# Talking-heads attention with a Fourier mix: the score and premix matmuls in 64x32 tiles, a new step order, and the order at the seam of two stages

## The chip, the cores and the metric

The kernel runs on one core of one Trainium2 chip. The metric is the device time of an execution in microseconds; each kernel is run several times and the median is compared. All data is float32.

## The reference, cut to what matters

```
B, NH, S, D = 8, 12, 448, 64
scores = q @ k.T / sqrt(D)                      # per batch and head, S x S
scores = einsum('bhij,hg->bgij', scores, w_pre) # premix: the 12 heads are mixed
attn   = softmax(scores, axis=-1)
attn   = einsum('bhij,hg->bgij', attn, w_post)  # postmix: mixed again
x      = (attn @ v), heads side by side         # B x S x 768
u      = x + real(fft(fft(x, axis=1), axis=2))
un     = (u - mean(u)) / sqrt(var(u) + 1e-6)    # over the last axis
out    = u + relu(un @ w_ch1) @ w_ch2           # 768 -> 3072 -> 768
```

## The kernel before, in words

There are two phases. `mix_phase` is the attention and the Fourier mix; `ffn_phase` is the norm and the two large products.

**The attention's step.** A batch is cut into 24 steps; there are TOT = 192 steps. Each step mixes 4 groups of 5 query rows, for all 12 heads (60 = KR rows on the partitions). The work of one row group passes through the following operations, several steps apart:

- `emit_qk` (L432): the scores of a block of query rows and two heads in each half of the array. They go to PSUM tiles `ms` and are copied by ScalarE to `Sb`. There is about one such group in every step.
- `emit_gather` (L451): four DMAs on SP's queue bring `Sb` into `Kr`, with heads and rows on the partitions. It runs LG = 4 steps ahead.
- `emit_premix` (L464): the first mixing, `Kr` times the constant `kw1`, into the PSUM tiles `mx`, LM = 2 steps ahead. There are four matmul calls in the four 64x64 quarters of the array.
- `emit_max` (L474) on VectorE, `emit_exp` (L481) on ScalarE, which also adds up the denominators, and `emit_scale` (L490) with the reciprocal on VectorE and the product on GpSimd.
- `emit_postmix` (L499): the second mixing, into `po`. There are eight matmul calls, each in a 64x32 piece of the array.
- `emit_turn` (L512): VectorE transposes `po` in 32x32 blocks into `Pv`.
- `emit_av` (L522): the product with v, 28 calls in 64x64 quarters, copied to `XT`. There are 12 in a batch.

Other work is called "full", because it uses the whole array: transposes of q and k (`emit_xpose`, L406), of the attention's output (`emit_x`, L558), and the two products of the Fourier mix, over rows (`emit_z`, L619) and over columns (`emit_s2`, L639). GpSimd's additions for the Fourier mix are lists of small functions called folds (`fold`, L574).

**What sets the order.** TensorE, VectorE, ScalarE and GpSimd carry out the loop at L750 in the order in which it is written. It calls, step by step: premix, flush (pending PSUM copies), postmix, maxima, exponentials, AV, turn, one operation of the weights' conversion (`wts.deal`), scores, gather, scale, pending stores, folds, full. The tables AT_T, AT_V, AT_QK, AT_AV, AT_X, AT_Z and AT_S (L77 to L85) say in which step of a batch each filling item is due; a step past the batch's end falls into the next batch. ENG (L87) says which engine copies what.

**The seam.** `ffn_phase` loads the first rows of `u` (L867) and the first weights `w1t` (L873). Then a hand-ordered section computes statistics (`stats`, VectorE), the root (`power`, four GpSimd operations, L897 to L900) and the folds left over (`fold_rest`). The next section normalises (`norm`, ScalarE, L908), transposes on TensorE (`turn`, L917, with copies on ScalarE, L919), subtracts (`total`, VectorE, which also issues seven stores of `ub`), and issues the `w2t` loads (L877). The first FFN round also carries the last "full" items between its matmuls. There are 42 rounds, each of `first` (L946) and `second` (L1002).

Of the kernel before, what the change touches and what calls it, by code (L numbers as in the profile page):

```python
# [10 lines left out]
F32 = mybir.dt.float32  # L11
U32 = mybir.dt.uint32
ALU = mybir.AluOpType
ACTF = mybir.ActivationFunctionType
AX = mybir.AxisListType

P = 128
# [13 lines left out]
KR = R * NH  # L31
# [42 lines left out]

AT_T = ((12, 10), (17, 16), (14, 18))  # L77
AT_L = ((-4, -3), (-2, -1), (0, 1), (2, 8), (12, 13), (14, 15))
AT_V = ((3, 4), (5, 6), (7, 7))
AT_QK = ((1, 2, 2), (0, 1, 2), (0, 1, 2), (0, 1, 2),  # L80
         (0, 1, 2), (0, 1, 2), (0, 1, 2), (0, 1, 2))
AT_AV = ((0, 2, 3), (1, 3, 5), (3, 4, 5), (1, 2, 3))
AT_X = (11, 20, 24, 29)
AT_Z = (38, 38, 41, 41)
AT_S = ((40, 44), (53, 55))  # L85

ENG = {("tr", "q", 4): "d", ("tr", "q", 3): "a", ("tr", "k", 4): "d",  # L87
       ("tr", "k", 3): "a", "QK": "aa", "AV": "aa", "X": "aa", "z": "a"}

# [193 lines left out]
def mix_phase(ctx, tc, rest, ident, q, k, v, w_pre, w_post, u_scr, u_rev, wts):  # L285
# [40 lines left out]
    def flush():  # L326
        while pend:
            pend.pop(0)[1]()
# [103 lines left out]
    def emit_qk(n, xx):  # L432

        bk = blocks[n]
        st = batches[bk["b"]]
        if xx == 0:
            bk["Sb"] = psb.tile([P, 6, S], F32, name="Sb", tag="Sb")
        r0 = bk["r0"]
        pss = [ms_tile() for _ in range(2)]
        for y in range(2):  # L440
            lo = r0 + MG * y
            for x in range(2):
                nc.tensor.matmul(  # L443
                    pss[x][64 * y:64 * y + r0 + 64 - lo, :S],
                    st["qT", xx][64 * x:64 * x + 64, y, lo:r0 + 64],
                    st["kT", xx][64 * x:64 * x + 64, y, :],
                    start=True, stop=True)
        return [lambda x=x: copy(ENG["QK"][x], bk["Sb"][:124, 2 * xx + x, :],
                                 pss[x][:124, :S]) for x in range(2)]

# [13 lines left out]
    def emit_premix(T):  # L464
        mx = [pmx.tile([P, 512], F32, name="mx", tag=f"mx{x}") for x in range(2)]
        Kr = steps[T]["Kr"]
        for x in range(2):
            for z in range(2):
                nc.tensor.matmul(mx[x][64 * z:64 * z + 64, :S],  # L469
                                 kw1[64 * x:64 * x + KR, :],  # L470
                                 Kr[64 * x:64 * x + KR, z, :], start=True, stop=True)
        steps[T]["mx"] = mx

    def emit_max(T):  # L474
        nmx = [psm.tile([P, 1], F32, name="nmx", tag=f"nmx{x}") for x in range(2)]
        for x in range(2):
            nc.vector.tensor_reduce(nmx[x][:, :], steps[T]["mx"][x][:, :S],  # L477
                                    axis=AX.X, op=ALU.max, negate=True)
        steps[T]["nmx"] = nmx

    def emit_exp(T):  # L481
        PP = ppp.tile([P, 2, S], F32, name="PP", tag="PP")
        den = psm.tile([P, 2], F32, name="den", tag="den")
        for x in range(2):
            nc.scalar.activation(PP[:, x, :], steps[T]["mx"][x][:, :S], ACTF.Exp,  # L485
                                 bias=steps[T]["nmx"][x][:, :],
                                 accum_out=den[:, x:x + 1])
        steps[T]["PP"], steps[T]["den"] = PP, den

    def emit_scale(T):  # L490
        PP, den = steps[T]["PP"], steps[T]["den"]
# [7 lines left out]
    def emit_postmix(T):  # L499
        po = ppo.tile([P, 2, 512], F32, name="po", tag="po")  # L500
        PP = steps[T]["PP"]
        for y in range(2):
            for c in range(2):
                for z in range(2):
                    o = 64 * y + 32 * c
                    nc.tensor.matmul(po[o:o + 32, z, :S],  # L506
                                     kw2[64 * z:64 * z + KR, y, :],
                                     PP[64 * z:64 * z + KR, :, c * HS:(c + 1) * HS],
                                     start=True, stop=True)
        steps[T]["po"] = po  # L510
# [11 lines left out]
    def emit_av(g, pr):  # L522

        st = batches[g["b"]]
        Pv = g["Pv"]
        rp = _row(Pv)
        nu = GT * 4
        pss = [ms_tile() for _ in range(2)]
        for jb in range(C7):
            for x in range(2):  # L530
                for y in range(2):
                    i = 2 * pr + x
                    nc.tensor.matmul(  # L533
                        pss[y][64 * x:64 * x + 64, :nu * R],
                        st["v", pr][64 * y:64 * y + 64, x, jb * D:(jb + 1) * D],
                        _ap(Pv, 64 * y * rp + 32 * jb + R * i,
                            [[rp, 64], [HS, nu], [1, R]]),
                        start=(jb == 0), stop=(jb == C7 - 1))
        if pr == 0:
            g["XT"] = pxt.tile([P, 6, XW], F32, name="XT", tag="XT")  # L540
        XT = g["XT"]
        rx = _row(XT)
        first, sg, none = PLACE[g["gi"]]

        def done(y):
            rs = _row(pss[y])
            for e in range(2):

                o = MG + first + sg * NB * e
                dst = _ap(XT, (3 * y + pr) * XW + o, [[rx, P], [sg * RS, R], [sg, RS]])  # L550
                src = _ap(pss[y], 60 * e, [[rs, P], [1, R], [R, RS]])
                copy(ENG["AV"][y], dst, src)
            if y == 1 and pr == 2:
                for o in none:
                    nc.gpsimd.memset(XT[:, :, MG + o:MG + o + 1], 0.0)
        return [lambda y=y: done(y) for y in range(2)]

    def emit_x(g):  # L558
# [190 lines left out]
    with tc.manual_schedule(engines={ET.PE, ET.DVE, ET.Activation, ET.Pool}):  # L749
        while s <= TOT - GS + AT_X[-1]:  # L750
            old = len(later)
            n = take("none", s)
            if 0 <= s + LM < TOT:
                emit_premix(s + LM)
            flush()
            if 0 <= s < TOT:
                emit_postmix(s)
            if 0 <= s + LM < TOT:
                emit_max(s + LM)
                emit_exp(s + LM)  # L760
            take("AV", s)
            if 0 <= s < TOT:
                emit_turn(s)
            if s >= 4:
                wts.deal(1)
            take("QK", s)
            if 0 <= s + LG < TOT:
                if any(e[2] is not None and e[2] <= (s + LG) // BS for e in pend):
                    flush()
                emit_gather(s + LG)  # L770
            if 0 <= s + LM < TOT:
                emit_scale(s + LM)
            for _ in range(old):
                later.pop(0)()
            for _ in range(min(len(folds), 1 if n and s > 3 else 2)):
                folds.pop(0)()
            take("full", s)
            s += 1
        flush()
        wts.deal(1000)  # L780
# [32 lines left out]
def ffn_phase(ctx, tc, rest, ident, u_scr, u_rev, wts, ub_scr, out, fold_rest,  # L813
# [61 lines left out]
    def load_w2(c, i):  # L875
        w2[i] = pw2.tile([P, FM, DH], F32, name="w2t", tag="w2t")
        nc.sync.dma_start(out=w2[i][:, :, :], in_=wts.w2[c][i])  # L877
# [33 lines left out]
    def turn(t, x):  # L911
        un = uns.pop(x)
        for y in range(2):
            ps = ps_tile("Q")
            for c in range(NK):
                cc = NK * y + c
                nc.tensor.transpose(ps[:, c * P:(c + 1) * P],  # L917
                                    un[:, cc * P:(cc + 1) * P], ident[:, :])
            nc.scalar.copy(  # L919
                out=ubs[t, UB[y, x // 2]][:, :, (x % 2) * P:(x % 2 + 1) * P],  # L920
                in_=ps[:, :NK * P].rearrange("p (c n) -> p c n", n=P))

    def total(t, n):
        o, a, b = ((4, 6, 0), (5, 2, 4), (6, 2, 6), (3, 1, 5))[n]
# [112 lines left out]
    with tc.manual_schedule(engines={ET.PE, ET.DVE}):  # L1037
        for x in range(NT2):
            norm(0, x)
            turn(0, x)  # L1040
        for n in range(4):
            total(0, n)
        for i in ORDER:
            load_w2(0, i)
        for n in range(NC * NTB):
            c, t = divmod(n, NTB)

            if c + 1 < NC and 0 <= t - (c == 0) < NK + FM:
                wts.add(c + 1, t - (c == 0))
            wts.deal(0)  # L1050
            if c == 0 and t + 2 < NTB:
                load_u(t + 2)
            second(n, first(n))
            wts.deal(1000)
            if n == 0:
                assert not parts
                rest.close()
                pu.append(pool("pu2", side="right"))
                beside.close()
                pps.append(pool("ppy", space=bass.MemoryType.PSUM))  # L1060
# [61 lines left out]
```

## Time and profile before

The median of 17 runs is 2426.83 us (2420.97 to 2434.74). The profiled execution took 2424.31 us; its span from first to last instruction is 2422.5 us, and the granted TensorE clock over it is 0.993 of full speed. The table gives busy times by stretch; PE is TensorE, DVE VectorE, ACT ScalarE, POOL GpSimd.

| stretch (us) | what runs | PE | DVE | ACT | POOL |
|---|---|---|---|---|---|
| 0 to 75 | first loads, first steps | 55.87 | 33.99 | 35.55 | 30.00 |
| 75 to 823 | attention steps | 743.82 | 593.41 | 521.05 | 552.45 |
| 823 to 867 | last steps, seam | 30.68 | 20.00 | 18.28 | 22.16 |
| 867 to 907 | first FFN round with the last mix items | 39.89 | 26.66 | 13.35 | 14.67 |
| 907 to the end | 41 FFN rounds | 1508.85 | 837.38 | 210.35 | 161.59 |

In a timeline line the first number is the start in us, the second the time to the end of the merged instructions, then come engine, source line, operation, output and inputs, shapes and count. Square brackets hold the idle time before it, and what ended that. Matmul ends are modelled, so starts are the safer reading.

### The profile page before, as it was taken

The numbers are of one execution on the slowest core, as the hardware profiler recorded it, in microseconds if no ns is written. First come the engines' busy times: TensorE is split into PE (matmuls) and PEld (weight loads), VectorE is DVE, ScalarE is ACT, GpSimd is POOL, SyncE is SP. The second block draws the span as 40 slices with busy tenths as digits, with TensorE's granted clock in tenths as the row PEclk, the third lists the DMA queues.
The fourth block names the chain that finished last, engine by engine and source line by source line (L and its number), as shares of the span: only waits on it lengthen the run. The fifth ranks groups of instructions, "written<-read, shape, count | busy, mean of one in ns | idle before, by whom it ended". The sixth has DMA issues, their size and how long they took to land.

```text
span 2422.5 us, 48510 instructions
## 1 busy us (share of the span) xinstructions
PE 2379.1 (98%) x18608; PEld 1551.7 (64%) x18608; DVE 1511.5 (62%) x3103; ACT 798.6 (33%) x2059; POOL 780.9 (32%) x1293
## 2 busy tenths in 40 slices
PE   6999999999999899999999999999999999999999
PEld 2445454454554477776777777777777777777776
DVE  3777778788787747785567356635665457533333
ACT  4777667666767542322111111111111110110110
POOL 3687877868676531121111011101110011000000
PEclk8999999999999999999999999999999999999999
DMA  6655554646554457346444444535443644353331
GB/s 146 175 182 162 179 171 155 200 157 191 168 167 146 162 202 215 124 151 232 147 136 153 143 145 135 157 116 170 143 150 98 200 127 146 121 167 114 118 117 52
DMA packets 168596, 372.10 MB, mean 154 GB/s; under 512 B 36750, under 2 KB 90022, under 8 KB 168366
## 3 DMA queue, kind: packets, MB, share of 16 engines
q1 hardware_dynamic: 129038, 260.22, 33.1%
q0 software_dynamic: 33760, 107.40, 15.3%
q8 instruction: 149, 2.44, 0.4%
q10 hardware_dynamic: 5568, 1.38, 0.3%
q14 instruction: 81, 0.66, 0.1%
HBM read 211.98 MB, written 74.34 MB: 118 GB/s over the span
## 4 chain that ended last, share of the span: by engine, by line
PE 94%; DMA 3%; SPq 1%; DVE 1%; ACT 1%; issue 0%; ACTq 0%; DVEq 0%
PE psP L946 18%; PE psP L1002 18%; PE psR L946 9%; PE psR L1002 9%; PE mx L469 7%; PE po L506 7%; PE ms L443 6%; PE ms L533 6%; PE psQ L1002 5%; PE psQ L946 4%; PE ms L647 2%; PE ms L420 2%; DMA Kr<-Sb 1%; PE ms L566 1%; PE ms L631 1%; PE psQ L917 1%
## 5 line engine op out<-in xcount | busy, mean ns | idle before, releaser
L946 PE MATMUL psP<-ub,w1t 128*128 128x256 f32 x2016 | 462.5, 379 | 0.0
L1002 PE MATMUL psP<-w2t,h 128*128 128x384 f32 x1344 | 461.0, 486 | 0.0
L946 PEld LDWEIGHTS psP<-ub,w1t 128*128 128x128 f32 x2016 | 382.8, 190 | 60.7
L207 POOL DMA_DIRECT2D raw<-in_moe_w_ch_dram x120 | 68.9, 574 | 924.5 <-DVE tmp L251 905.7
L1002 PEld LDWEIGHTS psP<-w2t,h 128*128 128x128 f32 x1344 | 254.4, 190 | 165.9
L496 POOL TENSOR_SCALAR PP<-PP,rcp 128x448 f32<-128x448 f32 x384 | 240.7, 636 | 235.6 <-DVE rcp L494 95.7
L477 DVE TENSOR_REDUCE nmx<-mx 128x1 f32<-128x448 f32 x384 | 222.4, 618 | 128.1 <-PE mx L469 125.6
L485 ACT ACTIVATE PP<-mx,nmx 128x448 f32<-128x448 f32 x384 | 240.1, 630 | 171.3 <-DVE nmx L477 159.5
L951 ACT COPY h<-psP 128x512 f32<-128x512 f32 x42 | 24.6, 586 | 764.4 <-PE psP L946 753.2
L1008 DVE TENSOR_TENSOR u<-u,psP 128x384 f32<-128x384 f32 x336 | 183.6, 553 | 141.3 <-PE psP L1002 139.1
L946 PE MATMUL psR<-ub,w1t 128*128 128x256 f32 x1008 | 231.3, 379 | 0.0
L469 PE MATMUL mx<-Kr,kw 60*64 60x448 f32 x1536 | 223.2, 553 | 7.6 <-DMA Kr<-Sb 6.2
L1002 PE MATMUL psR<-w2t,h 128*128 128x384 f32 x672 | 230.5, 486 | 0.0
L517 DVE STREAM_TRANSPOSE Pv<-po 128x896 f32<-128x896 f32 x192 | 212.8, 1108 | 8.7 <-PE po L506 7.5
L957 DVE TENSOR_TENSOR h<-h,psQ 128x512 f32<-128x512 f32 x42 | 28.9, 688 | 298.7 <-PE psQ L946 298.6
L946 PEld LDWEIGHTS psR<-ub,w1t 128*128 128x128 f32 x1008 | 191.4, 190 | 25.9
L324 ACT COPY Sb<-ms 124x448 f32<-124x448 f32 x384 | 184.8, 540 | 18.1 <-PE ms L443 6.4
L506 PE MATMUL po<-PP,kw 60*32 60x448 f32 x3072 | 188.7, 548 | 0.9 <-DVE rcp L493 0.9
L443 PE MATMUL ms<-kT,qT 64*64 64x448 f32 (+1 forms) x1536 | 188.6, 553 | 0.0
L533 PEld LDWEIGHTS ms<-Pv,vv 64*64 64x64 f32 x5376 | 143.8, 133 | 68.3 <-issue 30.7
L1002 PEld LDWEIGHTS psR<-w2t,h 128*128 128x128 f32 x672 | 127.2, 190 | 87.4
L533 PE MATMUL ms<-Pv,vv 64*64 64x120 f32 x5376 | 165.9, 269 | 0.0
(92 smaller groups left out, 2755.5 us busy)
## 6 DMA issues: line engine op xcount, KB each, us to landing
ub<-ub SPq DMA_DIRECT2D x294, 384.0 KB
Kr<-Sb SPq DMA_DIRECT2D x768, 105.0 KB
raw<-in_moe_w_ch_dram POOLq DMA_DIRECT2D x72, 256.0 KB, 3.3
raw<-in_moe_w_ch_dram POOLq DMA_DIRECT2D x48, 384.0 KB, 3.8
w<-wst POOLq DMA_DIRECT2D x126, 128.0 KB, 3.1
w<-wst POOLq DMA_DIRECT2D x84, 192.0 KB, 3.2
w1t<-w SPq DMA_DIRECT2D x42, 384.0 KB
w2t<-w SPq DMA_DIRECT2D x42, 384.0 KB
```

Of the source, the lines that this page charges most:

```text
L324: (nc.scalar.copy if eng == "a" else nc.vector.tensor_copy)(out=out, in_=in_)
L443: nc.tensor.matmul(pss[x][64 * y:64 * y + r0 + 64 - lo, :S], st["qT", xx][64 * x:64 * x + 64, y, lo:r0 + 64], st["kT", xx][64 * x:64 * x + ...
L469: nc.tensor.matmul(mx[x][64 * z:64 * z + 64, :S], kw1[64 * x:64 * x + KR, :], Kr[64 * x:64 * x + KR, z, :], start=True, stop=True)
L477: nc.vector.tensor_reduce(nmx[x][:, :], steps[T]["mx"][x][:, :S], axis=AX.X, op=ALU.max, negate=True)
L485: nc.scalar.activation(PP[:, x, :], steps[T]["mx"][x][:, :S], ACTF.Exp, bias=steps[T]["nmx"][x][:, :], accum_out=den[:, x:x + 1])
L496: nc.gpsimd.tensor_scalar(PP[:, x, :], PP[:, x, :], rcp[:, x:x + 1], 1.0, op0=ALU.mult, op1=ALU.mult)
L506: nc.tensor.matmul(po[o:o + 32, z, :S], kw2[64 * z:64 * z + KR, y, :], PP[64 * z:64 * z + KR, :, c * HS:(c + 1) * HS], start=True, stop=True)
L517: nc.vector.transpose(g["Pv"][:, T % GT, :].rearrange("p (z s) -> p z s", z=2), steps[T]["po"][:, :, :S])
L533: nc.tensor.matmul(pss[y][64 * x:64 * x + 64, :nu * R], st["v", pr][64 * y:64 * y + 64, x, jb * D:(jb + 1) * D], _ap(Pv, 64 * y * rp + 32 ...
L946: nc.tensor.matmul(p[:, m, :], w1[i][:, kc, m * P:(m + 1) * P], ub[:, kc, :], start=i in OPENS and m == kc == 0, stop=kc == NK - 1, skip_g ...
L1002: nc.tensor.matmul(p, lhs[i][:, kf, x * P:(x + 1) * P], w2[i][:, kf, :], start=i in OPENS and kf == 0, stop=kf == FM - 1, skip_group_check ...
L1008: nc.vector.tensor_tensor(us_, us_, p, op=ALU.add)
```

## The change

Five things are changed.

1. Each score and premix call is cut into two, each 32 columns of the array wide (the second piece of the half with 60 rows is 28 wide).
2. The due-step tables are written anew, and the copies of k's two halves change engines.
3. The step's order is read from two strings, one for even and one for odd steps. In both, premix and postmix are neighbours. In odd steps the scores come before AV. Maxima and exponentials are called one tile at a time. In the last three steps and after, no folds are called.
4. The zeroing of columns of `XT` goes from GpSimd to VectorE.
5. At the seam, the first transpose is pinned behind all that TensorE was given before, half of the first round's transposed pieces are copied by VectorE, and the `w2t` loads are issued ahead of the `ub` stores in `total`.

```diff
-AT_T = ((12, 10), (17, 16), (14, 18))
+AT_T = ((6, 10), (17, 18), (14, 16))
-AT_QK = ((1, 2, 2), (0, 1, 2), (0, 1, 2), (0, 1, 2),
+AT_QK = ((1, 2, 2), (0, 1, 2), (0, 1, 2), (1, 1, 2),
          (0, 1, 2), (0, 1, 2), (0, 1, 2), (0, 1, 2))
-AT_AV = ((0, 2, 3), (1, 3, 5), (3, 4, 5), (1, 2, 3))
+AT_AV = ((1, 2, 3), (0, 1, 5), (3, 4, 5), (1, 2, 4))
-AT_Z = (38, 38, 41, 41)
-AT_S = ((40, 44), (53, 55))
+AT_Z = (39, 39, 41, 41)
+AT_S = ((40, 44), (48, 54))
+ORDERS = tuple(o.split() for o in (
+    "conv pre post flush AV max0 exp0 "
+    "QK max1 exp1 turn scale full gather",
+    "pre post flush max0 max1 QK exp0 "
+    "AV turn exp1 scale gather conv full flush"))
...
-       ("tr", "k", 3): "a", "QK": "aa", "AV": "aa", "X": "aa", "z": "a"}
+ENG = {("tr", "q", 4): "d", ("tr", "q", 3): "a", ("tr", "k", 4): "a",
+       ("tr", "k", 3): "d", "QK": "aa", "AV": "aa", "X": "aa", "z": "a"}
...
+            for lo in (r0 + MG * y, r0 + MG * y + 32):
+                o = 64 * y + lo - r0 - MG * y
+                hi = min(lo + 32, r0 + 64)
+                for x in range(2):
+                    nc.tensor.matmul(
+                        pss[x][o:o + hi - lo, :S],
+                        st["qT", xx][64 * x:64 * x + 64, y, lo:hi],
+                        st["kT", xx][64 * x:64 * x + 64, y, :],
+                        start=True, stop=True)
...
+                for o in (0, 32):
+                    nc.tensor.matmul(mx[x][64 * z + o:64 * z + o + 32, :S],
+                                     kw1[64 * x:64 * x + KR, o:o + 32],
+                                     Kr[64 * x:64 * x + KR, z, :], start=True, stop=True)
...
-                    nc.gpsimd.memset(XT[:, :, MG + o:MG + o + 1], 0.0)
+                    nc.vector.memset(XT[:, :, MG + o:MG + o + 1], 0.0)
...
+                    if s < TOT - 3:
+                        for _ in range(min(len(folds), 1 if n and s > 3 else 2)):
+                            folds.pop(0)()
...
+                if t == x == y == c == 0:
+                    tc.keep_in_program_order(tr)
+            copy = nc.vector.tensor_copy if t == 0 and y else nc.scalar.copy
...
+        for i in ORDER:
+            load_w2(0, i)
         for n in range(4):
             total(0, n)
-        for i in ORDER:
-            load_w2(0, i)
```

More of the change, by code (lines that the diff above doesn't have):

```diff
@@ L72 @@
 NTB = B * S // TB
-AT_T = ((12, 10), (17, 16), (14, 18))
+AT_T = ((6, 10), (17, 18), (14, 16))
 AT_L = ((-4, -3), (-2, -1), (0, 1), (2, 8), (12, 13), (14, 15))
 AT_V = ((3, 4), (5, 6), (7, 7))
-AT_QK = ((1, 2, 2), (0, 1, 2), (0, 1, 2), (0, 1, 2),
+AT_QK = ((1, 2, 2), (0, 1, 2), (0, 1, 2), (1, 1, 2),
          (0, 1, 2), (0, 1, 2), (0, 1, 2), (0, 1, 2))
-AT_AV = ((0, 2, 3), (1, 3, 5), (3, 4, 5), (1, 2, 3))
+AT_AV = ((1, 2, 3), (0, 1, 5), (3, 4, 5), (1, 2, 4))
 AT_X = (11, 20, 24, 29)
-AT_Z = (38, 38, 41, 41)
-AT_S = ((40, 44), (53, 55))
-ENG = {("tr", "q", 4): "d", ("tr", "q", 3): "a", ("tr", "k", 4): "d",
-       ("tr", "k", 3): "a", "QK": "aa", "AV": "aa", "X": "aa", "z": "a"}
+AT_Z = (39, 39, 41, 41)
[7 more added lines that the diff above has]
+       ("tr", "k", 3): "d", "QK": "aa", "AV": "aa", "X": "aa", "z": "a"}
 NC = 6
@@ L440, in emit_qk @@
         for y in range(2):
[L441 to L447, printed above, removed]
+            for lo in (r0 + MG * y, r0 + MG * y + 32):
[7 more added lines that the diff above has]
+                        start=True, stop=True)
         return [lambda x=x: copy(ENG["QK"][x], bk["Sb"][:124, 2 * xx + x, :],
@@ L468, in emit_premix, with emit_max, emit_exp @@
             for z in range(2):
-                nc.tensor.matmul(mx[x][64 * z:64 * z + 64, :S],
-                                 kw1[64 * x:64 * x + KR, :],
-                                 Kr[64 * x:64 * x + KR, z, :], start=True, stop=True)
+                for o in (0, 32):
+                    nc.tensor.matmul(mx[x][64 * z + o:64 * z + o + 32, :S],
+                                     kw1[64 * x:64 * x + KR, o:o + 32],
+                                     Kr[64 * x:64 * x + KR, z, :], start=True, stop=True)
         steps[T]["mx"] = mx
[L474 to L488, printed above, removed]
+    def emit_max(T, x):
+        nmx = steps[T]["nmx", x] = psm.tile([P, 1], F32, name="nmx", tag=f"nmx{x}")
+        nc.vector.tensor_reduce(nmx[:, :], steps[T]["mx"][x][:, :S],
+                                axis=AX.X, op=ALU.max, negate=True)
+    def emit_exp(T, x):
+        if x == 0:
+            steps[T]["PP"] = ppp.tile([P, 2, S], F32, name="PP", tag="PP")
+            steps[T]["den"] = psm.tile([P, 2], F32, name="den", tag="den")
+        nc.scalar.activation(steps[T]["PP"][:, x, :], steps[T]["mx"][x][:, :S], ACTF.Exp,
+                             bias=steps[T]["nmx", x][:, :],
+                             accum_out=steps[T]["den"][:, x:x + 1])
     def emit_scale(T):
@@ L752, in mix_phase @@
             n = take("none", s)
[L753 to L768, printed above, removed]
-                    flush()
[L770 to L777, printed above, removed]
+            ahead, now = 0 <= s + LM < TOT, 0 <= s < TOT
+            for op in ORDERS[s % 2]:
+                if op == "flush":
+                    flush()
+                elif op in fill:
+                    take(op, s)
+                elif op == "conv":
+                    if s >= 4:
+                        wts.deal(1)
+                elif op == "gather":
+                    if 0 <= s + LG < TOT:
+                        if any(e[2] is not None and e[2] <= (s + LG) // BS for e in pend):
+                            flush()
+                        emit_gather(s + LG)
+                elif op == "scale":
+                    if ahead:
+                        emit_scale(s + LM)
+                    for _ in range(old):
+                        later.pop(0)()
+                    if s < TOT - 3:
+                        for _ in range(min(len(folds), 1 if n and s > 3 else 2)):
+                            folds.pop(0)()
+                elif op in ("post", "turn"):
+                    if now:
+                        (emit_postmix if op == "post" else emit_turn)(s)
+                elif ahead:
+                    (emit_premix if op == "pre" else emit_max if op[0] == "m"
+                     else emit_exp)(s + LM, *map(int, op[3:]))
             s += 1
@@ L916, in turn @@
                 cc = NK * y + c
[L917 to L921, printed above, removed]
+                tr = nc.tensor.transpose(ps[:, c * P:(c + 1) * P],
+                                         un[:, cc * P:(cc + 1) * P], ident[:, :])
+                if t == x == y == c == 0:
+                    tc.keep_in_program_order(tr)
+            copy = nc.vector.tensor_copy if t == 0 and y else nc.scalar.copy
+            copy(out=ubs[t, UB[y, x // 2]][:, :, (x % 2) * P:(x % 2 + 1) * P],
+                 in_=ps[:, :NK * P].rearrange("p (c n) -> p c n", n=P))
     def total(t, n):
```

## The prediction

> **What bounds the kernel now.** I read the busy table first, then the chain of waits, then the timeline of a few steps of the attention, then the seam. On the page TensorE covers the span, and the chain that ended last is TensorE's too:
>
> ```profile
> PE 2379.1 (98%) x18608; PEld 1551.7 (64%) x18608; DVE 1511.5 (62%) x3103; ACT 798.6 (33%) x2059; POOL 780.9 (32%) x1293
> PE 94%; DMA 3%; SPq 1%; DVE 1%; ACT 1%; issue 0%; ACTq 0%; DVEq 0%
> ```
>
> A busy TensorE may still lose time inside its busy spans, so I look at starts and not at ends. The timeline from 400 to 412 us shows the matmuls of a step (a call is two instructions here, so x8 is four calls):
>
> ```profile
> 401.61 0.30 PEld L443 LDWEIGHTS ms<-kT,qT 64*64 64x64 f32 x8
> 401.71 0.98 PE L443 MATMUL ms<-kT,qT 64*64 64x448 f32 x8
> 402.09 0.18 PEld L469 LDWEIGHTS mx<-Kr,kw 60*64 60x64 f32 x3 [0.18 <-issue]
> 402.46 1.01 PE L469 MATMUL mx<-Kr,kw 60*64 60x448 f32 x8
> ...
> 403.40 0.18 PEld L506 LDWEIGHTS po<-PP,kw 60*32 60x32 f32 x16 [0.70 <-POOL PP L496]
> 403.40 0.98 PE L506 MATMUL po<-PP,kw 60*32 60x448 f32 x16
> ...
> 404.32 0.20 PEld L443 LDWEIGHTS ms<-kT,qT 64*64 64x64 f32 x8 [0.73 <-ACT Sb L324]
> 404.32 0.98 PE L443 MATMUL ms<-kT,qT 64*64 64x448 f32 x8
> ...
> 405.23 1.56 PE L647 MATMUL ms<-tcs,z 97*112 97x193 f32 x8
> ```
>
> Read the differences of starts. Scores to premix, both 64x64 tiles: 402.46 - 401.71 = 0.75 us, and the premix's weights are loaded while the scores still run. Postmix to scores, 64x32 to 64x64: 404.32 - 403.40 = 0.92. Scores to the column product, 64x64 to the full array: 405.23 - 404.32 = 0.91. So **a change of tile shape costs 0.16 us** (0.91 - 0.75), in which the next weights wait for the array to empty.
>
> **The sum for a batch as it is.** A batch has 24 steps, each with a premix, a postmix and on average one score group: 72 x 0.75 = 54.0. With the other groups by their starts in the timeline less the change: 12 AV at 1.49, 6 transposes of q or k at 0.75, 4 of X at 0.66, 4 row products (z) at 0.80, 4 column products at 1.31: 87.4 in all. Changes of shape: two in every step (premix to postmix, postmix to what follows) and two more, in and out, in each step that holds a "full" item. By the table of due steps, modulo 24, those are steps 0, 5, 7, 10, 11, 12, 14, 16, 17, 18, 20: 48 + 22 = 70 changes, 11.2 us. Sum 98.6. The first postmix of batches 1 and 7 starts at 135.95 and 749.11, so a batch takes 613.2 / 6 = 102.2. Rows and count explain all but 3.6 us, the stalls before a premix or postmix.
>
> **Part 1: the tiles and the order.** Scores and premix issue 8 calls instead of 4, each half as wide. The postmix already is that form, 16 instructions, and takes 0.92 with its change, the same 0.75 without; its sixteen weight loads pass in 0.18. So I price a 64x32 group at 0.75, and what falls is the number of changes. After it, only AV and the full items differ in shape. AV falls in 12 steps (1, 2, 4, 7, 8, 9, 12, 13, 17, 21, 22, 23), the full items in 11 (0, 5, 6, 10, 11, 14 to 18, 20): two changes for each of the 23, less one in step 17, where AV meets a full item directly (odd steps put the scores ahead of AV): 45. Then 25 x 0.16 = **4.0 us a batch**. The six batches that the postmix starts bracket give 24.0. Batch 0 waits for transfers (TensorE is busy 55.9 of the first 75 us): I credit 2.5. Batch 7 thins out at its end: 3.0. Together 29.5.
>
> A rule speaks against this. The Trainium skill, "TensorE: Matmul & The Clock Gate", in the section on packing small matmuls, says that a weight load overlaps running matmuls only in another row group. Premix and postmix use the same row groups, so by the rule even neighbours of one shape would pay the drain, and the gain would be none. The rows at 402.09 and 402.46 contradict it for 64x64: same row groups, overlapped. No row has 64x32 behind 64x32, so bounds: 0 and 0.16 a succession; I take 0, by the 64x64 row and since the second pass within the postmix follows without a hole.
>
> **Part 2: what the table moves.** Halves of k change engine (ACT's 0.48 against DVE's 0.69, in 24 pairs), the zeroing of XT goes from POOL (0.11 each) to DVE, maxima and exponentials are interleaved with scores. VectorE is busy 80.7 of 100 us at 370 to 470, ACT 70, POOL 78: under TensorE's beat, so nil while TensorE sets it. Without that cover the stalls grow: the next premix waits until ScalarE has read its PSUM tile, and the gathers of one step occupy SP's queue 3.3 us (12 take 9.79). The shortest step of the old order has 2.6 us of TensorE work (step 4), of the new 3.1 (step 5), which speaks for fewer stalls; the steps are shorter on the whole, which speaks for more. I take the 3.6 as unchanged, bounds -2.5 and +3 a batch. In even steps the gather is issued behind the full item; its semaphores, not its place, decide when it runs: nil, the late Kr being within the same bounds.
>
> **Part 3: the seam.** From the timeline of 812 to 872 us:
>
> ```profile
> 841.41 0.47 PE L566 MATMUL ms<-ident,XT 128*113 128x128 f32 x2
> ...
> 843.88 1.94 POOL L587 TENSOR_TENSOR xs<-X 113x384 f32<-113x384 f32 x2
> ...
> 848.66 1.05 POOL L898 TENSOR_TENSOR mv<-mv,mhalf 128x4 f32<-128x4 f32 x1
> ...
> 850.36 1.95 ACT L908 ACTIVATE un<-u,mv 128x768 f32<-128x768 f32 x2 [10.64 <-POOL mv L900]
> ...
> 851.44 0.90 PE L917 MATMUL psQ<-ident,un 128*128 128x128 f32 x3 [9.56 <-ACT un L908]
> 852.69 1.20 PE L566 MATMUL ms<-ident,XT 128*113 128x128 f32 x4 [0.35 <-ACT XT L324]
> 853.82 6.53 PE L533 MATMUL ms<-Pv,vv 64*64 64x120 f32 x168
> ```
>
> TensorE stands for 9.56 us before the first FFN transpose: it needs the normed rows, they need the root on POOL (848.3 to 850.3), and the root stands behind eight fold operations (839.4 to 848.2). Behind the transpose stand three AV groups that need nothing of it. The change leaves the folds of the last steps until after the root and pins the transpose behind the attention. The statistics are done at 841.96, so the root ends at 844.0 instead of 850.3: 6.3 us. If ScalarE keeps the norms ahead of the XT copies that the X transposes (L566) wait for, TensorE is held that long and gains 6.3; if not, the whole hole of 9.6. Half of the 24 transposes' copies go to VectorE: before, the last 21 took 4.9 us (862.3 to 867.2) waiting for ScalarE: 0.7 off, bounds 0 and 1. I take 7.0, bounds 6.3 and 10.6. The moved folds run beside AV, and the first z follows X's copies about as far as now (863.1 to 878.9): nil, up to 2 if POOL is late. The seven w2 loads (3.6 us of SP) pass ahead of the ub stores; they are needed 13 us after today's issue, and the stores a whole round later: nil. The FFN behind 907 us, 1516 us, stays.
>
> **Sum.** 2424.3 (the profiled run; its span is 2422.5, the rest lies around it) - 29.5 - 7.0 = **2388**. The median of the runs, 2426.8, stands 2.5 above that run, which the range covers.
>
> **Rivals.** (a) *The 64x32 tiles drain at every succession* (the rule above). All 95 boundaries of a batch pay, 25 more than today: +4.0 x 7.4 batches = +29.5, less 7: **2447**, slower. It decides from 0.10 us a succession (36.5 / (50 x 7.4)). For it: the rule, and no such row. Against: the 64x64 row. 0.09.
> (b) *The short steps get another bound.* Eight new steps have 3.07 to 3.32 us of TensorE work; VectorE alone needs 80.7% of 102.2 / 24 = 3.44 a step. At a floor of 3.6 (that with 5% of waiting, an estimate) they lose 0.29 + 0.44 + 0.53 + 0.28 + 0.37 + 0.28 + 0.28 + 0.44 = 2.9 a batch, 21.5 in all: **2409**. For it: SP's and VectorE's shares. Against: slack from long steps lies between. 0.19.
> (c) *The stalls fall too*, since no step is as short as 2.6 any more: two thirds of 3.6 over 7.4 batches, 18 more: **2370**. 0.14.
> The forecast has 0.58. That the order isn't carried out as written is possible only at the seam (the two values of part 3).
>
> **Numbers.** The forecast's own bounds run some 14 down and 20 up; the range 2366 to 2411 takes in (b) and (c), and leaves out (a) and tails. A measurement here tells about 0.2%, 4.9 us, from no change. Faster 0.90 (all but (a) and a sliver of (b)), same 0.02, slower 0.08.
>
> **What would show it.** Right: premix to postmix starts 0.75 apart, postmix to scores 0.75; a batch near 98 us; no hole of over 4 us on TensorE at the seam. Wrong: those starts at 0.91 (rival a); 0.75 but premixes waiting for ScalarE or gathers, VectorE over 90% (b); if batches take 95 or less, (c).

## The result, and the profile after

The changed kernel takes 2407.65 us (median of 8 runs, 2403.02 to 2410.75), against 2426.94 for the kernel before in the same comparisons. The ratio is 0.9917, with a 95% interval from 0.9905 to 0.9929. The forecast was 2388 with a range from 2366 to 2411: the direction and the range held, but the gain is 19 us where the sum had 36.5.

The busy table and the first line of the chain of waits:

```profile
PE 2358.4 (98%) x21680; PEld 1590.9 (66%) x21680; DVE 1548.6 (64%) x3139; ACT 797.3 (33%) x2055; POOL 789.4 (33%) x1261
...
PE 89%; DMA 4%; SPq 2%; DVE 2%; ACT 1%; issue 1%; POOL 0%; ACTq 0%; DVEq 0%; POOLq 0%
```

TensorE is still busy 98% of the span, but its share of the chain fell from 94% to 89%, and transfers and SP's queue rose. This is the first sign that the attention now waits on transfers. The share of busy time does not show it.

The timeline of a step near 805 us has the starts that the prediction asked to look at (the lines of other engines are left out):

```profile
805.41 0.98 PE L478 MATMUL mx<-Kr,kw 60*32 60x448 f32 x16
...
806.19 0.96 PE L512 MATMUL po<-PP,kw 60*32 60x448 f32 x16
...
806.94 0.96 PE L451 MATMUL ms<-kT,qT 64*32 64x448 f32 x16
...
807.83 1.56 PE L653 MATMUL ms<-tcs,z 97*112 97x193 f32 x8
```

Premix to postmix is 0.78, postmix to scores 0.75, and scores to the full-array product 0.89. Groups of one shape follow each other without the 0.16 us, also for 64x32, which no row of the trace before had shown.

The spans divide as follows. Batches are counted between their first postmixes. The tail is from batch 7's first postmix to the last postmix, the seam from there to the first FFN matmul.

| part of the span | before | after | change | forecast |
|---|---|---|---|---|
| up to batch 1's first postmix | 135.9 | 136.0 | 0.0 | -2.5 |
| batches 1 to 6 | 613.2 | 608.3 | -4.9 | -24.0 |
| batch 7 to its last postmix | 89.7 | 87.2 | -2.5 | -3.0 |
| seam | 28.4 | 18.5 | -9.9 | -7.0 |
| FFN | 1555.3 | 1555.6 | +0.3 | 0 |

Nearly all that is missing is in batches 1 to 6. To split it, I take for each of the 24 steps its shortest duration in batches 2 to 6, and call what lies above it in batches 1 to 6 a loss. (Where a step of batch 1 is shorter still, its loss is put at nothing.) The shortest steps add up to 99.5 us a batch before and 95.6 after: 3.9 less, where the count of shape changes gave 4.0. Counted in the matmuls of the traces, the shape changes 69 times a batch before (from batch 2 on) and 45 times after. The losses went from 3.1 to 6.25 us a batch. So **the saved changes of shape arrived and most of them were given back as new waits**: 6 x 3.9 = 23.5 less 6 x 3.15 = 18.9 is 4.6, beside the 4.9 of the table; the rest is rounding and the short steps of batch 1.

Which waits? The summed idle times of the weight loads in batches 1 to 6, first before, then after (total us, times, longest):

```profile
PEld mx L469 <- ACT PP L485: 9.3, 27, 0.6
...
PEld mx L469 <- DMA Kr<-Sb: 8.0, 15, 2.2
```

```profile
PEld mx L478 <- DMA Kr<-Sb: 22.6, 28, 2.6
...
PEld mx L478 <- ACT PP L492: 12.5, 37, 1.4
...
PEld mx L478 <- ACT XT L330: 5.6, 17, 2.0
```

The premix's weight loads wait almost three times as long for the gathered rows Kr. The waits for ScalarE grew too: those for the exponentials that read the premix's PSUM tile (PP) by 3.2 us, and 5.6 us more are put down to copies of XT. The timeline of the changed kernel at 429 to 437 us shows one wait for Kr in place:

```profile
427.29 9.95 SPq L467 DMA_DIRECT2D Kr<-Sb  x10
...
434.32 1.00 PE L478 MATMUL mx<-Kr,kw 60*32 60x448 f32 x12
...
436.06 0.14 PEld L478 LDWEIGHTS mx<-Kr,kw 60*32 60x32 f32 x4 [1.54 <-DMA Kr<-Sb]
436.06 0.57 PE L478 MATMUL mx<-Kr,kw 60*32 60x448 f32 x2 [0.74 <-DMA Kr<-Sb]
...
436.16 0.97 ACT L330 COPY Sb<-ms 124x448 f32<-124x448 f32 x2 [2.83 <-PE mx L478]
```

Twelve of the premix's sixteen instructions start at 434.32; the last four wait for one of the four gathers. The chain of waits gives that transfer's time:

```profile
429.89 6.13 DMA Kr<-Sb
```

Its issue began at 429.89, and it landed 6.13 us after that. From the records of all gathers at 75 to 815 us I worked out the time from the end of issue on SP to the last byte, with the packets counted off to the gathers in the order of their starts: the median is 1.84 us in both kernels, but the slowest tenth begins at 2.90 before and at 3.65 after. Up to the last step of the semaphore that the premix waits for (a counter that a transfer raises as it lands), the median is 2.7 us in both, and the slowest tenth begins at 4.1 before and 5.2 after.

The seam, from the timeline:

```profile
833.76 1.05 POOL L908 TENSOR_TENSOR mv<-mv,mhalf 128x4 f32<-128x4 f32 x1
...
835.47 1.95 ACT L918 ACTIVATE un<-u,mv 128x768 f32<-128x768 f32 x2 [3.15 <-POOL mv L910]
...
837.80 0.72 PE L572 MATMUL ms<-ident,XT 128*113 128x128 f32 x4 [2.02 <-ACT XT L330]
...
838.45 4.93 PE L539 MATMUL ms<-Pv,vv 64*64 64x120 f32 x168
...
845.49 0.82 PE L927 MATMUL psQ<-ident,un 128*128 128x128 f32 x6
```

The root no longer stands behind the folds, and the AV groups run before the FFN's first transpose. TensorE's hole of 9.56 us is now 2.02 us. ScalarE did keep the norms ahead of the XT copies, which is why these 2 us remain.

### The profile page after: what moved, and what is told of

Its sections match the earlier page's. It is cut to its first block, busy times and chain, and to the rows that moved or that the text cites. A ratio compares the mean times of both kernels' runs of the same rounds, so it can differ in the third digit from the quotient of the medians.

```text
span 2405.5 us, 54666 instructions
## 1 busy us (share of the span) xinstructions
PE 2358.4 (98%) x21680; PEld 1590.9 (66%) x21680; DVE 1548.6 (64%) x3139; ACT 797.3 (33%) x2055; POOL 789.4 (33%) x1261
## 4 chain that ended last, share of the span: by engine, by line
PE 89%; DMA 4%; SPq 2%; DVE 2%; ACT 1%; issue 1%; POOL 0%; ACTq 0%; DVEq 0%; POOLq 0%
PE psP L960 18%; PE psP L1016 18%; PE psR L960 9%; PE psR L1016 9%; PE mx L478 6%; PE ms L451 5%; PE ms L539 5%; PE po L512 5%; PE psQ L1016 5%; PE psQ L960 5%; DMA Kr<-Sb 3%; PE ms L653 2%; SPq L467 2%; PE ms L426 1%; PE ms L637 1%; PE ms L572 1%
## 5 line engine op out<-in xcount | busy, mean ns | idle before, releaser
L502 POOL TENSOR_SCALAR PP<-PP,rcp 128x448 f32<-128x448 f32 x384 | 254.1, 671 | 218.3 <-DVE rcp L500 165.3
L485 DVE TENSOR_REDUCE nmx<-mx 128x1 f32<-128x448 f32 x384 | 222.8, 617 | 95.6 <-PE mx L478 94.1
L478 PE MATMUL mx<-Kr,kw 60*32 60x448 f32 x3072 | 235.1, 547 | 18.5 <-DMA Kr<-Sb 13.5
L512 PE MATMUL po<-PP,kw 60*32 60x448 f32 x3072 | 212.6, 538 | 3.0 <-DVE rcp L499 1.7
L451 PE MATMUL ms<-kT,qT 64*32 64x448 f32 (+1 forms) x3072 | 203.9, 542 | 0.7 <-DVE wrp L366 0.7
```

Source lines behind the costliest of these rows:

```text
L451: nc.tensor.matmul(pss[x][o:o + hi - lo, :S], st["qT", xx][64 * x:64 * x + 64, y, lo:hi], st["kT", xx][64 * x:64 * x + 64, y, :], start=Tr ...
L478: nc.tensor.matmul(mx[x][64 * z + o:64 * z + o + 32, :S], kw1[64 * x:64 * x + KR, o:o + 32], Kr[64 * x:64 * x + KR, z, :], start=True, sto ...
L485: nc.vector.tensor_reduce(nmx[:, :], steps[T]["mx"][x][:, :S], axis=AX.X, op=ALU.max, negate=True)
L502: nc.gpsimd.tensor_scalar(PP[:, x, :], PP[:, x, :], rcp[:, x:x + 1], 1.0, op0=ALU.mult, op1=ALU.mult)
L512: nc.tensor.matmul(po[o:o + 32, z, :S], kw2[64 * z:64 * z + KR, y, :], PP[64 * z:64 * z + KR, :, c * HS:(c + 1) * HS], start=True, stop=True)
```

## The experiments

All ratios below are against the kernel before, in the same comparison. "Lost" is the loss a batch as defined above, in batches 1 to 6.

**The seam alone** (the changes of `turn`, of the folds' condition and of the w2 loads put into the kernel before):

```diff
+            if s < TOT - 3:
...
+                if t == x == y == c == 0:
+                    tc.keep_in_program_order(tr)
+            copy = nc.vector.tensor_copy if t == 0 and y else nc.scalar.copy
```

> The kernel before with the seam's edits alone (folds of the last steps held back, first transpose pinned, half the copies on VectorE, w2 loads first). If the seam is a part of its own, the time from the last postmix to the first FFN matmul falls from 28.4 to about 18.5 us as in the changed kernel, and the median to about 2417. If the seam only gained because the attention's end had changed too, less: above 2421.

2421.61 us, ratio 0.9985 (0.9971 to 0.9999). The seam took 22.0 us instead of 28.4; the rest of its profiled run was as before within a microsecond or two. So the seam's edits gain 6.4 us by themselves in this trace; the medians differ by 3.5, and the time is in the second of the two cases expected. The remaining 3.5 of the 9.9 came only with the attention's new end: in this run TensorE still stood for 3.9 us before the X transposes.

**The tiles alone** (scores and premix in 64x32 in the kernel before, as in the change's diff).

> The kernel before with scores and premix in 64x32 tiles, old tables, old order, old seam. By my count this alone takes the shape changes from 70 to 45 a batch. Theory G (the saved time is given back in waits for the gathered rows Kr): premix to postmix starts 0.75 to 0.78 apart, but stalls grow by about as much as in the changed kernel; 2417 to 2422. Theory T (the new tables and order caused the extra stalls): about 2405 and below. If the tiles gain nothing without the order: 2427.

2419.98 us, ratio 0.9983 (0.9966 to 1.0). The shortest steps fall to 96.9 a batch, the losses rise to 5.2. Batches 1 to 6 gain 2.8 us. The extra stalls come with the shorter steps, also in the old order, as theory G had it. The waits of the premix for Kr and for ScalarE both doubled:

```profile
PEld mx L472 <- ACT PP L488: 20.2, 49, 1.3
PEld mx L472 <- DMA Kr<-Sb: 18.2, 27, 2.3
```

The shape changes 45 times a batch here too, but the shortest steps fell by 2.6 and not by 4.0: a wait that comes back in every batch is no loss by this measure, so 5.2 is likely too low.

**The order and tables with the old tiles** (the changed kernel, with 64x64 scores and premix):

```diff
-                for o in (0, 32):
-                    nc.tensor.matmul(mx[x][64 * z + o:64 * z + o + 32, :S],
-                                     kw1[64 * x:64 * x + KR, o:o + 32],
+                nc.tensor.matmul(mx[x][64 * z:64 * z + 64, :S],
+                                 kw1[64 * x:64 * x + KR, :],
```

> The changed kernel with scores and premix in 64x64 tiles again: new tables, new order, new seam. Shape changes are 70 a batch as before. Theory G: with the longer steps the gathers are in time again; attention as long as before or a little shorter, the seam's 10 us stay: 2413 to 2418. Theory T (the tables make stalls of their own): attention longer than before, 2420 and above.

2419.19 us, ratio 0.9977 (0.9962 to 0.9992). The seam is at 19.1. Batches 1 to 6 take 615.5 us, 2.3 more than before, with 4.0 lost: the new tables have no gain in the attention by themselves. With the tiles they are worth something: the changed kernel is 11.5 us below this one, while the tiles in the old order gain 5 (medians). The four kernels side by side:

| | before | tiles alone | order and tables, old tiles | both |
|---|---|---|---|---|
| lost a batch, us | 3.1 | 5.2 | 4.0 | 6.25 |
| premix waits for Kr, batches 1 to 6, us | 8.0 | 18.2 | 10.8 | 22.6 |
| slowest tenth of landings from, last byte, us | 2.90 | 3.00 | 3.60 | 3.65 |
| the same, last step of the semaphore, us | 4.1 | 4.6 | 4.9 | 5.2 |

Two things add up. With the new order and tables alone the gathers land later, but the waits for them grow by 2.8 us only. With the tiles alone the landings grow less and the waits more than double; what differs there is that the steps are shorter. So the landings alone do not set the waits.

**Gathers called a step earlier:**

```diff
-    LG, LM = 4, 2
+    LG, LM = 5, 2
```

> The changed kernel with the gathers called one step earlier (five steps ahead of the postmix instead of four). Theory G: the premix's weight loads wait less for Kr (25.6 us at 75 to 815 us of the changed kernel), and the time falls by 5 to 13 us, to 2395 to 2403. Theory V (a floor of VectorE and ScalarE holds the short steps): no difference, 2406 to 2410. If SP's queue is the limit and not the time of the call: no difference either.

2409.87 us, ratio 0.9934 (0.9918 to 0.9951): no gain, and the premixes waited 22.9 us for Kr. The gathers did not run earlier: from the first issue of a step's gather to its premix passed 8.0 us in the median, against 7.9 in the changed kernel. The place of the call does not set when a gather runs, as the prediction had it. For the first step of each block of rows the trace shows what does: its first gather is issued 0.03 us (median) after the copy of the block's last scores into Sb.

**Loads left out.** Batches 1 to 7 reuse q, k and v tiles of batch 0, so 210 transfers are gone and the output is not the reference's:

```diff
+        if b:
+            batches[b]["raw" + nm, xx] = batches[0]["keep" + nm, xx or 1]
+            return True
...
+        if b:
+            batches[b]["v", pr] = batches[0]["v", pr]
+            return
```

> The changed kernel with q, k and v loaded in batch 0 alone; the later batches reuse tiles of batch 0, so the output is not the reference's. TensorE, VectorE and ScalarE do the same work; GpSimd's queue issues 210 transfers less. Theory L (the gathers land late because these loads share the 16 transfer engines): the slowest tenth of landings falls from over 3.6 us to under 2.5, premix waits for Kr (22.6 us in batches 1 to 6) fall below 8, and the time falls by 12 to 25 us, to 2383 to 2396. Theory V (VectorE and ScalarE are the floor of the short steps): landings fall but the time by under 5 us.

The same in the kernel before:

> The kernel before with the same loads left out. Theory L: it gains as well, but less, since its longer steps covered most late landings: 3 to 12 us; the difference between the two kernels then grows from 19 us to 27 to 37, near the forecast's 36.5. Theory V: the difference stays at 19.

| | changed | with loads once | before | with loads once |
|---|---|---|---|---|
| median, us | 2407.65 | 2387.9 | 2426.94 | 2409.11 |
| batches 1 to 6, us | 608.3 | 591.3 | 613.2 | 603.0 |
| lost a batch, us | 6.25 | 3.30 | 3.10 | 1.09 |
| slowest tenth of landings from, us | 3.65 | 2.32 | 2.90 | 2.01 |

The ratios are 0.9824 (0.9796 to 0.9852) and 0.9917 (0.9891 to 0.9944). The same view as above, for the changed kernel with loads once:

```profile
PEld mx L484 <- DMA Kr<-Sb: 7.9, 11, 2.8
```

The wait for Kr falls from 22.6 to 7.9 us, as expected of theory L. But the whole kernel before gains almost as much as the changed one, 18 against 20 us, so the expectation for the difference of the medians (27 to 37) failed: it is 21. Within batches 1 to 6 the difference between the kernels does grow, from 4.9 to 11.7 us, but the seam took 22.7 us in the changed kernel with loads once, 4.2 more than with them, and 28.3, as before, in the other. (TensorE stood for 2.05 us in the middle of the last AV groups there, for no cause that the profile shows.) The shortest steps are 99.8 and 95.7 us a batch in these two runs, 4.1 apart. Of the 18.9 us of added losses there, the loads account for 6 x (3.15 - 2.21) = 5.6 us by these figures, and 13 us stay. The edit also takes the issue of those loads off GpSimd (about 0.72 us each for q and k), so it isn't purely a test of the transfers: a late GpSimd is a rival that no run tests by itself.

**Half the bytes of the gathers:**

```diff
-                    out=Kr[64 * x:64 * x + KR, z, :],
-                    in_=_ap(Sb, p0 * row, [[RS * row, 2 * R], [S, 6], [1, S]]))
+                    out=Kr[64 * x:64 * x + KR, z, :HS],
+                    in_=_ap(Sb, p0 * row, [[RS * row, 2 * R], [S, 6], [1, HS]]))
```

> The changed kernel with the gathers moving 224 of 448 columns; the premix reads these twice, so its result differs from the reference's. SP issues as many transfers with as many rows, of half the bytes. If the gathers' own bytes make them late: landings shorten, 6 to 15 us less. If the loads in front of them on the engines or the issue time on SP make them late: under 5 us less.

2394.74 us, ratio 0.9855 (0.9829 to 0.9882), 13 us below the changed kernel. The median landing falls to 1.34 us, the slowest tenth begins at 2.28, and the premixes wait 7.7 us for Kr. Batches 1 to 6 gain 5.8 us, and batch 1 begins 5.8 us earlier. Late gathers are thus shown to cost time in two ways: less traffic beside them helps, and fewer bytes in them help. Neither takes all of the losses away (5.1 a batch here). The premixes' wait for Kr fell by 14.9 us and batches 1 to 6 by 5.8: where the gather is in time, another wait often stands behind it, so the length of a wait in such a list is not what its removal is worth.

**More VectorE work, more ScalarE work**, one small operation in each step:

```diff
+        nc.vector.tensor_scalar(rcp[:, :], rcp[:, :], 1.0, None, op0=ALU.mult)
```

> The changed kernel with one more small VectorE operation per step (a multiplication of the reciprocals by 1, about 0.17 us, between the reciprocal and GpSimd's scaling; 192 of them, 33 us of VectorE). Theory V: a floor on VectorE would pass on most of it in the short steps, 10 to 25 us more. Theory L: VectorE has slack; under 5 us more.

```diff
+        if x == 0:
+            nc.scalar.copy(out=mk[:, 0, :], in_=mk[:, 1, :])
```

> The changed kernel with one more small ScalarE copy per step (128 x 5 elements, about 0.2 us, between the two exponentials; 192 of them, 38 us of ScalarE; what it copies alters nothing that is used later). If ScalarE's order (copies, then exponentials, which free the premix's PSUM tiles) holds the short steps, 10 us or more are passed on; if the gathers alone hold them, under 5 us.

2408.27 us, ratio 0.9917 (0.9890 to 0.9944), and 2407.75 us, ratio 0.9925 (0.9908 to 0.9942). VectorE's busy time rose by 23.6 us (1548.6 to 1572.2), ScalarE's by 16.4 (797.3 to 813.7), 0.12 and 0.09 us a step (less than the 0.17 and 0.2 expected), and none of it can be seen in the total. The busy time of neither engine is the floor of the short steps.

**q and k loads in other steps:**

```diff
-AT_L = ((-4, -3), (-2, -1), (0, 1), (2, 8), (12, 13), (14, 15))
+AT_L = ((-8, -7), (-6, -5), (-4, -4), (0, 1), (8, 9), (15, 16))
```

> The changed kernel with the q and k loads called in other steps of the batch (16 to 20, 0, 1, 8, 9, 15, 16 instead of 20 to 23, 0 to 2, 8, 12 to 15), where the steps are long or lost nothing. Theory L (loads in front of the gathers): the losses of steps 10 to 14 and 21 to 23 shrink, 3 to 12 us less than the changed kernel. If only the amount of loading counts and not its place: no difference.

2408.36 us, ratio 0.9915 (0.9899 to 0.9932). Losses fall to 5.25 a batch, and batches 1 to 6 gain 2.1 us, but batch 1 begins 7.8 us later, since the same table also sets the order at the start. Inconclusive.

**The reversed half stored in one transfer.** SP's queue stands once a batch, because the last row of a reversed half is stored by a transfer that must wait for the indirect one (timeline of the changed kernel, SP's queue):

```profile
267.57 3.26 SPq L467 DMA_DIRECT2D Kr<-Sb  x4
273.91 0.23 SPq L682 DMA_DIRECT2D v<-X  x1
274.57 9.84 SPq L467 DMA_DIRECT2D Kr<-Sb  x12
```

Gathers that could have run stand behind that store. The edit lets the indirect transfer take 113 rows instead of 112:

```diff
-                            ap=rows[:GR, pair:pair + 1], axis=0),
-                        in_=X[:GR, :], in_offset=None)
-                    if pair:
-                        nc.sync.dma_start(out=u_rev[b][GR:GR + 1, :], in_=X[GR:GR + 1, :])
+                            ap=rows[:n, pair:pair + 1], axis=0),
+                        in_=X[:n, :], in_offset=None)
```

> The changed kernel with the last row of the reversed half stored by the indirect transfer itself, instead of by a second transfer on SP's queue that waits for it. Today SP stands there once a batch, 270.9 to 273.9 us in batch 2, and the gather behind it starts at 274.6, four us before its premix. Theory Q (this wait in SP's queue makes part of the stalls): steps 11 to 14 lose less, 6 to 14 us less than the changed kernel. If the gathers had slack there: under 3 us.

> The two edits above together. If the stalls are late gathers of both kinds, the gains add up: 10 to 22 us less than the changed kernel, to 2386 to 2398.

Slower: 2460.32 us, ratio 1.0138 (1.0121 to 1.0155), and with the moved loads 2462.07, ratio 1.0129 (1.0099 to 1.0159). The traffic line of the page, of the changed kernel and then of this one:

```profile
DMA packets 168620, 372.50 MB, mean 155 GB/s; under 512 B 36750, under 2 KB 90022, under 8 KB 168366
```

```profile
DMA packets 175387, 372.54 MB, mean 152 GB/s; under 512 B 43582, under 2 KB 96854, under 8 KB 175134
```

There are 6,832 more small packets, 840 of 8 bytes in each of the eight transfers of 113 rows. But the rows themselves did not go in small pieces. The packet records show them as 56 packets of 6,144 bytes and one of 3,072, one after the other, with never more than two in flight: 380.8 to 399.8 us for the one issued at 377.55. In the changed kernel the 112 rows of the same batch go as 48 packets of 6,144 bytes and 16 of 3,072, up to 16 at once: 372.0 to 374.4 us. A gather issued during the long store, and the premix behind it, wait (chain of waits of this run):

```profile
386.12 15.14 DMA Kr<-Sb
```

The semaphore of this gather makes its last step but one at 390.49 us, and the last at 401.26, after the store has ended. Steps 10 and 11, in the middle of the batches, take 3.7 and 3.8 us longer (medians). The edit was meant to test SP's wait and can't: it put a worse transfer in its place. What it does show is how directly a gather that lands late becomes TensorE's time. Whether SP's wait for the row store makes part of the remaining losses stays open.

## Why the prediction was right or wrong, point by point

- **TensorE as the bound, a shape change at 0.16 us, 70 changes to 45:** right. The traces have 69 and 45. The shortest steps fell by 3.9 us a batch (4.1 with the loads left out), forecast 4.0. The rule of the Trainium skill ("TensorE: Matmul & The Clock Gate", in the part on packing small matmuls) that a weight load overlaps only with another row group did not hold for 64x32 either: 0.75 to 0.78 between groups that share row groups. Rival (a) is out.
- **"I take the 3.6 as unchanged, bounds -2.5 and +3 a batch":** this is the step that failed. The losses rose by 3.15 a batch, just over the upper bound, and took 18.9 of 24 us. The prediction saw SP's 3.3 us a step and the gather's wait, and priced them at nothing. What was mis-sized, for a part of it, is the room of the gather. From the copy of a block's last scores to the block's first premix passed 7.7 us in the median before and 7.3 after, at the least 6.2 and 5.3; the four issues (0.81 us each) and the slowest landing must fit in. With the tiles alone the landings grew least and the waits for Kr more than doubled; the new order made the landings later. How much of the 18.9 us this is stays open. The loads left out account for 5.6, and halving the gathers' bytes gave 5.8 back. The rest was not traced to a cause; waits for ScalarE rose beside those for Kr.
- **Batch 0, 2.5 us:** wrong, nothing. It gained 4.9 us with loads once and 5.8 with half gathers; the run with more ScalarE work is 2.6 below too, so a difference of that size between single traces means little there.
- **Rival (b), 2409 us:** the time is right, and half of what it said. Of its signs, premixes that wait for gathers and ScalarE came; VectorE over 90% did not (85% from 75 to 815 us). Its sum stands on a floor at 3.6 us a step, and that is wrong: steps 18 and 19 ran in 3.33 and 3.01 us in every batch from 1 to 6, and more work on VectorE or ScalarE cost nothing.
- **The range:** it held at its edge. The time is 20 us above the forecast, as far as the forecast's own bounds went, in the part that the range took in for (b).
- **The seam, 7.0 with bounds 6.3 and 10.6:** 9.9. The mechanism is as told, with ScalarE's order as feared. 6.4 comes from the seam's edits alone; with the attention's new end the statistics' root ended at 835.4 us, 4.0 after the last postmix, against 11.5 before.
- **Everything priced at nothing** (k's halves, zeroing, w2 loads, folds after the root): no sign of a cost; between the first matmuls of the first and the second FFN round lie 49.1 us in both.
- **Still open:** the losses that stay when the loads are left out, 3.3 us a batch against 1.1 of the kernel before. The gathers' own bytes and ScalarE's copies and exponentials are candidates with a measurement each, SP's wait for the row store and GpSimd are candidates without one, and no run removed more than one.

## What to carry to other kernels

When the bounding engine gets faster by a known count, check the slack of every transfer that it waits for at the new pace, not at the old one: issue time on its queue, plus the slowest tenth of its landings, against the shortest stretch between producer and consumer. Waits that total little in the profile before may be just covered. To find the share that came back as waits, compare the shortest duration of each repeated step with its mean; the first shows what the edit did, the second what the surroundings took, except for waits that come back every time, which stay in the shortest.

## What the runs showed of the hardware that was not expected

- Gathers between two places in SBUF (105 KB, 60 rows of 1,792 bytes) took 1.84 us to land in the median, but the slowest tenth over 3.65 us; without the q, k and v loads in the same stretch of time it was 2.32.
- An indirect transfer of 113 rows of 3,072 bytes moved its packets one after the other and took 18 to 20 us; one of 112 rows moved up to 16 at once, and the one looked at took 2.4 us. One such long transfer a batch, with the gathers behind it, cost the kernel 50 us in all.
- 64x32 matmul groups of 16 instructions follow each other at 0.75 us, as fast as 64x64 groups of 8; doubling the instructions of scores and premix (18,608 to 21,680 matmuls in all) cost nothing that can be seen.
